# A decay floor moved into the scan, a fourth place for first loads, and four smaller edits in a gated-attention and two-MLP kernel

## The chip, the cores and the metric

The kernel runs on one core of a Trainium2 chip. A core has a matrix engine (TensorE, PE in the profile, with its weight loads shown apart as PEld), a vector engine (DVE), a scalar engine (ACT), a third engine (GpSimd, POOL) and a queue engine (SyncE, SP) that issues the DMA transfers here. The metric is device time in microseconds (us) of one execution of the whole program, lower is better. The time before is the median of three runs.

## The reference, cut to what matters

```python
def _attn_ref(q, k, v, alpha):              # q, k, v, alpha: 4 x 8 heads x 768 x 48
    for t in range(S):
        state = alpha[:, :, t, :, None] * state + np.einsum('bhd,bhe->bhde', k[:, :, t], v[:, :, t])
        y[:, :, t] = np.einsum('bhd,bhde->bhe', q[:, :, t], state)

def _moe_ref(x, mu_k, mu_r, w_k, w_v, w_r): # x: 4 x 768 x 384, w_k: 384 x 1024
    xk = mu_k * x + (1.0 - mu_k) * x_prev   # x_prev: x one token earlier
    xr = mu_r * x + (1.0 - mu_r) * x_prev
    k = np.maximum(xk @ w_k, 0.0)
    return sigmoid(xr @ w_r) * (k * k @ w_v)

def _moe2_ref(x, U, V, w_ch1, w_ch2):       # w_ch1: 384 x 1536
    u = x + (x.transpose(0, 2, 1) @ U @ V).transpose(0, 2, 1)
    return u + np.maximum(u @ w_ch1, 0.0) @ w_ch2
```

The three stages follow one another. The weights arrive as 64-bit floats; q, k, v and alpha as 32-bit.

## The kernel before

**Blocks.** The 4 x 768 tokens are cut into eight blocks of 384 tokens. A block goes through attention, then the first MLP (`moe1`); after all eight, the second MLP (`moe2`) goes through the eight blocks again. Every large product is done as three matmuls on a high and a low part of each operand (`mm3`), 384 columns wide; these are the 128x384 matmuls of the profile.

**Attention.** A block holds two units, a unit two phases (`ph`), a phase two heads: one head on partitions 0 to 47 (`EV`), the other on 64 to 111 (`OD`), together `BOTH` = 0 to 111. The time axis is cut into chunks of 128 tokens. `prep` (line 700) turns alpha into running products with two scans on DVE: a backward one into `G` and a forward one into `Fp`. Between them stands a floor: POOL takes the maximum of the three chunk starts of `G` and `DECAY_MIN` into `aC` (line 712), DVE takes its reciprocal into `bt` (line 713), and the second scan starts from that. Then come the transposes of the decayed keys (`keys_by_token`, PE, line 310), the score matmuls (`scores`), the state matmuls (`states`) and the outputs (`outputs`), whose results ACT copies into the block's `x`.

**The first block.** `first_attention` (line 826) does unit 1 before unit 0. Each phase is loaded into one of three places `T[0]` to `T[2]`; `tile_of` gives phases 2, 3, 0, 1 the places 0, 1, 2, 0, so the fourth load has to wait until the first phase is used up. The rows of x that don't fit a unit's own 96 partitions are spread by six small DMAs of 16 x 384 (`outputs`, `spread`), which read what unit 1 wrote. The copies of unit 0's outputs write all of rows 0 to 111, and so also the rows 48 to 63 that the spread fills; a spread DMA therefore comes after them.

**Weights.** `w_k` is loaded in pieces of 128, 256, 384, 128 and 128 columns into `raw` places, decoded by ACT and DVE to 32 bits (line 596), and split into high and low parts. `w_v`, `w_r` and the later weights go through four such places in turn, so a load waits until its place has been decoded.

**Results.** At the end of a block of `moe2`, DVE adds each of three 128-token results into a place of a ring of two (`x2_ring`) and SP sends it out: the third addition waits until the first result has left.

**What sets the order.** The kernel doesn't leave the order to the program text. `Plan` collects every operation with its operands and an assumed cost, and `schedule` (line 186) simulates five engines, each taking the ready operation of best priority; the priorities come from the table `DUE` and then from passes backward over the result (`issue`). Each engine runs its list strictly in that order. Where the simulation sees PE idle, it puts matmuls on a zero tile `warm` (128x128, line 395) that compute nothing; once placed, PE has to execute them. An assumed cost that is changed for one kind of operation (here the cost of a DMA, line 365) can therefore move instructions anywhere in the program.

## Time and profile before

| | |
|---|---|
| median of 3 runs | 724.15 us (722.25 to 725.62) |
| the profiled execution | 724.62 us, its span from first to last instruction 722.9 us |
| PE busy | 705.5 us (98%), 5319 instructions |
| DVE busy | 508.5 us (70%) |
| ACT busy | 354.5 us (49%) |
| POOL busy | 75.8 us (10%) |
| mean granted clock of PE | 0.992 |
| chain that ended last | PE 74%, DVE 6%, ACT 4%, DMA 3% |
| HBM | 43.85 MB read, 9.44 MB written |

A profile is one execution. Busy time of PE counts the matmuls on the zero tile too, so a PE that is busy 98% is not one that does useful work 98% of the time. In the timeline a row gives the start, the length, the engine, the source line, the operation with its output and input, the number of instructions merged into it, and in brackets how long the engine was idle just before and what ended that.

### The profile page before, as it was taken

To read this page: it belongs to the slowest core of one execution; us is meant where nothing else is said; L and a number is where in the kernel's file an instruction comes from. 1 tells how busy PE (TensorE), PEld (TensorE's weight loads), DVE (VectorE), ACT (ScalarE), POOL (GpSimd) and SP (SyncE) were. 2 spreads that over 40 slices of the span, in tenths; PEclk is the share of its full clock that TensorE was granted. 3 is DMA by queue.
4 is the path that set the end of the run, shared out by engine and by line. 5 is a ranking of instruction groups with operands and counts; after the bars stand their busy time and mean duration, and the time that the engine had idled before them with its cause. 6 is when DMAs were issued, how large, how long until landed. Compare 5 with 4: busy or idle time off the path is not lost.

```text
span 722.9 us, 13907 instructions
## 1 busy us (share of the span) xinstructions
PE 705.5 (98%) x5319; PEld 675.4 (93%) x5319; DVE 508.5 (70%) x1173; ACT 354.5 (49%) x901; POOL 75.8 (10%) x131
## 2 busy tenths in 40 slices
PE   7999999999999999999999999999999999999995
PEld 7798889899999999999999999999999999999995
DVE  6898987897776567773699999575665657474611
ACT  2588656976767557677797672212121112111210
POOL 2021101442130311311002100000000000000000
PEclk9999989999999999999999999999999999999998
DMA  8835733434333222313253240102020202020001
GB/s 222 200 102 157 186 84 102 108 94 109 85 98 75 63 62 60 98 51 99 65 153 110 66 143 16 51 0 66 1 67 1 65 1 67 1 66 2 34 1 37
DMA packets 29484, 55.46 MB, mean 77 GB/s; under 512 B 5344, under 2 KB 20064, under 8 KB 29408
## 3 DMA queue, kind: packets, MB, share of 16 engines
q1 hardware_dynamic: 29408, 54.48, 27.3%
q8 instruction: 43, 0.70, 0.4%
q14 instruction: 33, 0.27, 0.1%
HBM read 43.85 MB, written 9.44 MB: 74 GB/s over the span
## 4 chain that ended last, share of the span: by engine, by line
PE 74%; DVE 6%; ACT 4%; DMA 3%; issue 1%; SPq 1%; DVEq 0%; ACTq 0%
PE bank L305 73%; DMA arena<-in_qka_dram 3%; ACT arena L320 2%; DVE arena L137 2%; DVE arena L982 2%; DVE rounded L137 1%; PE bank L310 1%; SPq L366 1%; ACT rounded L320 1%; DVE shared L137 1%; ACT shared L320 1%; DMA out_dram<-arena 0%; ACT bank L320 0%; DVE shared L349 0%; DVEq L137 0%
## 5 line engine op out<-in xcount | busy, mean ns | idle before, releaser
L305 PE MATMUL bank<-rounded 128*128 128x384 f32 x2232 | 424.3, 339 | 2.9 <-ACT rounded L320 1.2
L305 PEld LDWEIGHTS bank<-rounded 128*128 128x128 f32 x2232 | 383.7, 186 | 13.2 <-ACT arena L320 2.2
L305 PE MATMUL bank<-rounded,shared 128*128 128x384 f32 x864 | 164.9, 335 | 0.8 <-DVE rounded L137 0.5
L320 ACT ACTIVATE rounded<-bank 128x384 fp32r<-128x384 f32 x160 | 78.3, 489 | 175.4 <-PE bank L305 174.3
L305 PEld LDWEIGHTS bank<-rounded,shared 128*128 128x128 f32 x864 | 150.9, 188 | 1.7 <-DVE rounded L137 1.0
L320 ACT ACTIVATE arena<-arena 128x384 f32<-128x384 f32 (+6 forms) x234 | 103.2, 463 | 48.2 <-DMA arena<-in_qka_dram 29.4
L137 DVE SCALAR_TENSOR_TENSOR rounded<-bank,rounded 128x384 fp32r<-128x384 f32 x96 | 53.4, 556 | 91.4 <-ACT rounded L320 90.3
L982 DVE STREAM_TRANSPOSE arena<-arena 32x96 f32<-32x96 f32 x384 | 103.8, 270 | 5.7
L305 PE MATMUL bank<-shared 128*48 128x128 f32 (+3 forms) x1472 | 100.3, 266 | 3.4 <-DMA shared<-in_v_dram 1.2
L305 PEld LDWEIGHTS bank<-shared 128*48 128x48 f32 (+2 forms) x1472 | 86.6, 142 | 17.8 <-issue 6.2
L320 ACT ACTIVATE rounded<-arena 128x384 fp32r<-128x384 f32 (+2 forms) x137 | 70.4, 522 | 63.6 <-DVE arena L982 49.4
L137 DVE SCALAR_TENSOR_TENSOR arena<-arena 128x384 int32<-128x384 int32 (+2 forms) x140 | 79.9, 590 | 8.9 <-ACT arena L320 8.3
L320 ACT ACTIVATE bank<-bank 128x384 f32<-128x384 f32 x128 | 61.6, 482 | 23.4 <-PE bank L305 22.7
L137 DVE TENSOR_TENSOR rounded<-arena,rounded 128x384 fp32r<-128x384 f32 (+1 forms) x108 | 60.5, 570 | 11.4 <-ACT rounded L320 10.9
L137 DVE TENSOR_TENSOR arena<-bank,arena 128x384 f32<-128x384 f32 (+1 forms) x76 | 41.5, 552 | 25.0 <-PE bank L305 9.9
L137 DVE TENSOR_TENSOR rounded<-bank,rounded 128x384 fp32r<-128x384 f32 x64 | 35.4, 552 | 30.6 <-ACT rounded L320 28.9
L320 ACT ACTIVATE arena<-bank 112x384 f32<-112x384 f32 (+3 forms) x76 | 37.3, 504 | 35.2 <-PE bank L305 33.3
L137 DVE TENSOR_TENSOR shared<-bank,arena 128x384 f32<-128x384 f32 x64 | 33.9, 547 | 24.5 <-PE bank L305 23.0
L137 POOL TENSOR_TENSOR rounded<-arena,rounded 128x384 fp32r<-128x384 f32 (+1 forms) x25 | 27.7, 1116 | 110.5 <-ACT rounded L320 110.4
L395 PE MATMUL bank<-warm 128*128 128x128 bf16 x581 | 37.4, 224 | 1.1 <-DVE arena L543 1.1
L395 PEld LDWEIGHTS <-warm 128*128 128x128 bf16 x581 | 34.5, 101 | 3.1 <-issue 1.5
L349 DVE TENSOR_TENSOR_SCAN shared<-arena 128x384 f32<-128x384 f32 x32 | 31.0, 967 | 4.4 <-ACT arena L320 4.3
(47 smaller groups left out, 258.3 us busy)
## 6 DMA issues: line engine op xcount, KB each, us to landing
arena<-in_qka_dram SPq DMA_DIRECT2D x56, 216.0 KB, 3.7
arena<-in_w_dram SPq DMA_DIRECT2D x24, 384.0 KB, 3.5
shared<-in_v_dram SPq DMA_DIRECT2D x32, 144.0 KB, 3.0
x2d<-arena SPq DMA_DIRECT2D x24, 192.0 KB, 2.2
arena<-x2d SPq DMA_DIRECT2D x8, 576.0 KB, 4.1
out_dram<-arena SPq DMA_DIRECT2D x24, 192.0 KB, 1.9
arena<-in_w_v_dram SPq DMA_DIRECT2D x8, 384.0 KB, 3.2
arena<-in_qka_dram SPq DMA_DIRECT2D x24, 72.0 KB, 2.0
```

The costliest lines, as they stand in the source:

```text
L137: fn(**args)
L305: "PE", cost, [out], [lhsT, rhs], lambda out, lhsT, rhs: fn(out, lhsT=lhsT, rhs=rhs, start=start, stop=stop),
L310: self.add("PE", cost, [out], [in_, ident], lambda: self.nc.tensor.transpose(out, in_, ident))
L320: self.add("ACT", cost, outs, [in_] + extra, lambda out, in_: fn(out, in_, func, **kw), out=out, in_=in_)
L349: lambda: self.nc.vector.tensor_tensor_scan(out=out, data0=d0, data1=d1, initial=0.0, op0=ALU.mult, op1=ALU.add), True,
L366: lambda: self.nc.sync.dma_start(out, in_),
L395: lambda i: nc.tensor.matmul(banks[SPARE[i]][:, 384:512], lhsT=warm, rhs=warm, start=True, stop=True), FILL_UNTIL, ROUNDS
L982: plan.dve(284, [to], [src], lambda to=to, src=src: nc.vector.transpose(out=to, in_=src))
```

## The change

Six edits, and the order that the planner makes of them:

- **Floor in the scan.** `ends` holds `DECAY_MIN` instead of zero off the chunk ends, the first element of a chunk is set to zero, and the backward scan takes the maximum where it took the sum. The result is already floored, so POOL's maximum and `aC` go: 32 instructions of line 712.
- **A fourth place.** `T[3]` lies on raw places 2 and 3. Phase 1 is loaded there, behind no other phase. All of `prep` now works on rows 0 to 111, so the second head is loaded with 48 rows instead of 64.
- **Outputs head by head.** In the first block unit 0's outputs are copied for each head alone (four copies of 48 x 384 on ACT instead of two of 112 x 384), which leaves the spread rows alone; the six spread DMAs now follow unit 1.
- **Smaller pieces.** `w_k` comes in pieces of 128, 128, 384, 128, 128 and 128 columns. Three are loaded from the start (four before), the last three later, and the due numbers `wk1` to `wk5` change.
- **Three result places.** `moe2` writes its results into `rs`, which has three places.
- **The planner's DMA cost** is the number of words over 56 instead of over 90.

The zero-tile matmuls in the program are 599 after, 581 before; PE's other instructions are the same 4001 matmuls in another order. Up to the first 128x384 matmul PE has 263 zero-tile matmuls now and had 325; between the first six 128x384 matmuls and the next transposes it has 240 and had 188.

```diff
@@ -41,7 +41,7 @@
 
 DUE = dict(
     slot1=2.01, end1=62, end2=81, end=28, keys=6.0, prep=1.66, load=52, mix_r=65, mix_k=44, mix0_r=61,
-    mix0_k=468, wk0=-238, wk1=-283, wk2=-17, wk3=45, wk4=60, wkk=7, wv=-12, r0=5, wr=37, early=31, x2=25, u=48, w1=227,
+    mix0_k=468, wk0=-238, wk1=-230, wk2=-220, wk3=38, wk4=45, wk5=60, wkk=7, wv=-12, r0=5, wr=37, early=31, x2=25, u=48, w1=227,
     w1s=-9, w2=23, pu=144, s_w="ACT DVE", s_lo="DVE", s_w1="ACT DVE", s_lo1="DVE",
     d1="ACT", d2="ACT", d="ACT", m0="DVE", m1="DVE", m="DVE", ut="DVE", ul="DVE",
     e0="DVE DVE", e1="DVE DVE", e2="DVE DVE", e="DVE POOL",
...
@@ -343,11 +343,11 @@
             self.nc.vector.tensor_scalar, True, out=out, in0=in0, scalar1=s1, scalar2=s2, **ops,
         )
 
-    def scan(self, out, d0, d1):
+    def scan(self, out, d0, d1, op=ALU.add):
         self.add(
             "DVE", 66.0 + 2.085 * out.free_size(), [out], [d0, d1],
             lambda: self.nc.vector.tensor_tensor_scan(
-                out=out, data0=d0, data1=d1, initial=0.0, op0=ALU.mult, op1=ALU.add
+                out=out, data0=d0, data1=d1, initial=0.0, op0=ALU.mult, op1=op
             ), True,
         )
 
...
@@ -362,7 +362,7 @@
         for d in out.shape:
             words *= d
         self.add(
-            "SP", max(cost, words / 90.0), [out if out_key is None else out_key], [in_ if in_key is None else in_key],
+            "SP", max(cost, words / 56.0), [out if out_key is None else out_key], [in_ if in_key is None else in_key],
             lambda: self.nc.sync.dma_start(out, in_),
         )
 
...
@@ -457,6 +457,7 @@
     Xs = [None, None]
     Xs[0] = new(KD + 1, TB + 1)
     raw_at = [words(arena, 2 * TB) for _ in range(4)]
+    T.append(view(arena, raw_at[2], (KD * TB + 1,)))
     raw_n = [0]
     rs_at = words(arena, NT * DM)
     rs = view(arena, rs_at, (NT, DM))
...
@@ -493,7 +494,6 @@
     KV = new(2, D, NC)
     carry = new(2, 2, D)
     G, Fp, bt = (att(TB) for _ in range(3))
-    aC = new(NC)
     w1h, w1l = (view(shared, i * KD * DF2, (KD, DF2), F32R) for i in range(2))
     last_w2 = [view(shared, 2 * KD * DF2 + i * DM, (DM,), F32R) for i in range(2)]
 
...
@@ -547,11 +547,12 @@
     plan.pool(600, [ident], [], lambda: make_identity(nc, ident))
 
     def make_ends():
-        nc.vector.memset(ends, 0.0)
+        nc.vector.memset(ends, DECAY_MIN)
         nc.vector.memset(ends[:, CH - 1 :: CH], 1.0)
 
     plan.dve(480, [ends], [], make_ends)
     plan.dve(400, [bt], [], lambda: nc.vector.memset(bt, 0.0))
+    plan.pool(60, [low], [], lambda: nc.gpsimd.memset(low, 0.0))
 
     def make_tri():
         nc.gpsimd.memset(tri, 1.0)
...
@@ -673,7 +674,7 @@
         return u // 4, (u // 2) % 2, (u % 2) * 2
 
     def tile_of(ph):
-        return T[{2: 0, 3: 1, 0: 2, 1: 0}[ph] if ph < 4 else ph % 3]
+        return T[{2: 0, 3: 1, 0: 2, 1: 3}[ph] if ph < 4 else ph % 3]
 
     def load_qka(ph, parts=((0, KD),), rows=D, to=None):
 
...
@@ -683,9 +684,10 @@
         for a, z in parts:
             for hh in range(2):
                 src = qka[b, h0 + hh, half, 0, a, 0]
+                n = D if hh else rows
                 plan.dma(
-                    t[64 * hh : 64 * hh + rows, a * TB : z * TB],
-                    bass.AP(src.tensor, src.offset, [[KD * TB, rows], [1, (z - a) * TB]]), in_key="in", cost=475.0,
+                    t[64 * hh : 64 * hh + n, a * TB : z * TB],
+                    bass.AP(src.tensor, src.offset, [[KD * TB, n], [1, (z - a) * TB]]), in_key="in", cost=475.0,
                 )
 
     def load_v(u):
...
@@ -694,30 +696,29 @@
             plan.dma(VS[u % 2][:, eo].rearrange("p c j d -> p (c j d)"), v[b, p0 // 2, half, eo], in_key="in")
 
     def check_pair(ph, t):
-        there = junk[:, 0 : t.free_size()].rearrange("p (c t) -> p c t", c=t.shape[1])
-        plan.act(there, t, AF.Relu, scale=-1.0, bias=ALPHA_MIN, accum_out=low[:, ph : ph + 1])
+        there = junk[BOTH, 0 : t.free_size()].rearrange("p (c t) -> p c t", c=t.shape[1])
+        plan.act(there, t, AF.Relu, scale=-1.0, bias=ALPHA_MIN, accum_out=low[BOTH, ph : ph + 1])
 
     def prep(ph, due, engs):
 
-        qt, kt, at = q_k_a(tile_of(ph))
-        g0, f, a0 = G[:, 0:TB:CH], fc[:, ph, :], firsts[:, ph, :]
+
+        qt, kt, at = (t[BOTH] for t in q_k_a(tile_of(ph)))
+        g, fp, f, a0, first = G[BOTH], Fp[BOTH], fc[BOTH, ph, :], firsts[BOTH, ph, :], at[:, 0:TB:CH]
         if ph >= CHECK_LATER:
             plan.at = due + 10
             check_pair(ph, at[:, 0:TB].rearrange("p (c t) -> p c t", t=CH)[:, :, 1:])
         plan.at = due
-        first = at[:, 0:TB:CH]
         plan.act(a0, first, AF.Copy)
-        plan.act(first, ends[:, 0:NC], AF.Copy)
-        plan.scan(G[:, ::-1], at[:, 1 : TB + 1][:, ::-1], ends[:, ::-1])
-        plan.pool(160, [aC], [g0], lambda: nc.gpsimd.tensor_scalar_max(out=aC, in0=g0, scalar1=DECAY_MIN))
-        plan.dve(110, [bt], [aC], lambda: nc.vector.reciprocal(bt[:, 0:TB:CH], aC))
-        plan.pool(163, [f], [a0, g0], lambda: nc.gpsimd.tensor_tensor(out=f, in0=a0, in1=g0, op=ALU.mult))
+        plan.act(first, ends[BOTH, 0:NC], AF.Copy, scale=0.0)
+        plan.scan(g[:, ::-1], at[:, 1 : TB + 1][:, ::-1], ends[BOTH, ::-1], ALU.max)
+        plan.dve(90, [bt], [g], lambda: nc.vector.reciprocal(bt[BOTH, 0:TB:CH], g[:, 0:TB:CH]))
+        plan.pool(163, [f], [a0, g], lambda: nc.gpsimd.tensor_tensor(out=f, in0=a0, in1=g[:, 0:TB:CH], op=ALU.mult))
         plan.at = due + 6
-        plan.scan(Fp, at[:, 0:TB], bt)
+        plan.scan(fp, at[:, 0:TB], bt[BOTH])
         plan.at = due + 14
-        plan.tt(KB[ph % 2], kt, G, ALU.mult, engs[0])
+        plan.tt(KB[ph % 2][BOTH], kt, g, ALU.mult, engs[0])
         plan.at = due + 17
-        plan.tt(QG[ph % 4], qt, Fp, ALU.mult, engs[1])
+        plan.tt(QG[ph % 4][BOTH], qt, fp, ALU.mult, engs[1])
 
     def scores(ph, due):
 
...
@@ -767,7 +768,8 @@
         if not half:
             plan.act(last, R[BOTH, :, :, NC - 1], AF.Copy)
 
-    def outputs(u, due, spread):
+    def outputs(u, due, spread, apart=False):
+
 
 
         b, half, p0 = unit(u)
...
@@ -788,7 +790,8 @@
                         else:
                             plan.mm(y, st[BOTH, h, j, c, :], QG[ph % 4][BOTH, cs], False, True, plan.S128)
         for j in range(2):
-            plan.act(x[BOTH, p0 + j, 1:], two_b[j][BOTH, 0:TB], AF.Copy)
+            for r in (EV, OD) if apart else (BOTH,):
+                plan.act(x[r, p0 + j, 1:], two_b[j][r, 0:TB], AF.Copy)
         if spread:
             for kk in range(KD):
                 for a in (0, 64):
...
@@ -840,7 +843,7 @@
                 keys_by_token(ph, due + 20 * j + 8)
                 scores(ph, due + 20 * j + 9)
             states(u, due + 25)
-            outputs(u, due + 30, i == 1)
+            outputs(u, due + 30, i == 0, i == 1)
 
 
     mm_at = [0]
...
@@ -1017,7 +1020,7 @@
         second(NF2 - 1)
         for t in range(NT):
             plan.at = mm_at[0] - EARLY + 4 * t
-            o = x2_ring()
+            o = rs[:, t, :]
             plan.tt(o, acc[t], u[:, t, :], ALU.add)
             tok = half * TB + t * P
             plan.dma(out[b, tok : tok + P, :], o, out_key=f"out{n}{t}")
...
@@ -1054,9 +1057,9 @@
     load_mu()
     c0 = 0
     for i, (n, at) in enumerate(
-        ((P, raw_at[0]), (2 * P, raw_at[1]), (3 * P, rs_at), (P, raw_at[3]), (P, raw_at[0]))
+        ((P, raw_at[0]), (P, raw_at[1]), (3 * P, rs_at), (P, raw_at[2]), (P, raw_at[3]), (P, raw_at[0]))
     ):
-        raw = load_weight(w_k[:, :, c0 : c0 + n], at, -1650 if i < 4 else DUE["wk4"] - 60)
+        raw = load_weight(w_k[:, :, c0 : c0 + n], at, -1650 if i < 3 else DUE[f"wk{i}"] - 60)
         for j in range(0, n, P):
             plan.at = DUE[f"wk{i}"] + DUE["wkk"] * (j // P)
             cs = slice(c0 + j, c0 + j + P)
```

On SP's queue at the start, before (`in_qka` are loads of q, k and alpha of one head, the widths 384, 768 and 1152 a part or all of the three; `in_v`, `in_mu`, `in_w_k` the other inputs; `arena<-arena` a spread DMA):

```order
L366 DMA arena<-in_qka_dram 64x1152 x2
L366 DMA shared<-in_v_dram 128x288 x3
L366 DMA arena<-in_qka_dram 64x1152 x2
L366 DMA shared<-in_v_dram 128x288
L366 DMA arena<-in_w_k_dram 128x3x256
L366 DMA arena<-in_w_k_dram 128x3x512
L366 DMA arena<-in_mu_dram 128x6
L366 DMA arena<-in_qka_dram 48x1152 x2
L366 DMA arena<-in_w_k_dram 128x3x768
L366 DMA arena<-arena 16x384 x3
```

and after, from the same place (behind the eight loads of phases 2 and 3):

```order
L366 DMA shared<-in_v_dram 128x288 x2
L366 DMA arena<-in_qka_dram 64x1152
L366 DMA arena<-in_qka_dram 48x1152
L366 DMA arena<-in_qka_dram 64x1152
L366 DMA arena<-in_qka_dram 48x1152
L366 DMA shared<-in_v_dram 128x288 x2
L366 DMA arena<-in_w_k_dram 128x3x256 x2
L366 DMA arena<-in_mu_dram 128x6
L366 DMA arena<-in_w_k_dram 128x3x768
L366 DMA arena<-arena 16x384 x6
```

The first two loads of v now go ahead of phase 0, phase 1 follows phase 0 directly, and all six spread DMAs stand in one row, ahead of the late pieces of `w_k`.

On DVE at the first phase, before (`SCALAR_TENSOR_TENSOR` of line 349 is a scan, line 137 the product with k or q):

```order
L349 SCALAR_TENSOR_TENSOR shared<-arena 128x384
L137 TENSOR_TENSOR shared<-arena,shared 128x384
L713 RECIPROCAL shared<-arena 128x3
L349 SCALAR_TENSOR_TENSOR shared<-arena,shared 128x384
L349 SCALAR_TENSOR_TENSOR shared<-arena 128x384
```

and after:

```order
L349 SCALAR_TENSOR_TENSOR shared<-arena 112x384
L714 RECIPROCAL shared<-shared 112x3
L137 TENSOR_TENSOR shared<-arena,shared 112x384
L349 SCALAR_TENSOR_TENSOR shared<-arena,shared 112x384
L349 SCALAR_TENSOR_TENSOR shared<-arena 112x384
```

The reciprocal reads the scan's own output and stands right behind it; the product comes third.

On PE at the end of the program, before (`bank0`, `bank1` and `bank2` collect the three results of the last block, `shared2` holds the last row of the second weight, so the row with it ends a result):

```order
L305 MATMUL bank0_73<-shared2_4057,rounded_71 128x384 x3
L305 MATMUL bank1_74<-rounded_71 128x384 x3
L305 MATMUL bank2_75<-rounded_71 128x384 x3
L305 MATMUL bank1_74<-rounded_71 128x384 x3
L305 MATMUL bank2_75<-rounded_71 128x384 x2
L305 MATMUL bank1_74<-shared2_4057,rounded_71 128x384 x3
L305 MATMUL bank2_75<-rounded_71 128x384
L305 MATMUL bank2_75<-shared2_4057,rounded_71 128x384 x3
```

and after:

```order
L305 MATMUL bank0_73<-shared2_4048,rounded_71 128x384 x3
L305 MATMUL bank1_74<-rounded_71 128x384
L305 MATMUL bank2_75<-rounded_71 128x384
L305 MATMUL bank1_74<-shared2_4048,rounded_71 128x384 x3
L305 MATMUL bank2_75<-rounded_71 128x384 x2
L305 MATMUL bank2_75<-shared2_4048,rounded_71 128x384 x3
```

The first result is complete with 10 matmuls still to come instead of 15.

On PE in the second block's attention, before (128x128 with `bank6` or `bank7` are scores of one head, three chunks; `bank0` to `bank2` products of the first MLP):

```order
L305 MATMUL bank6_79<-shared_72 128x128 x3
L305 MATMUL bank0_73<-rounded_71 128x384
L305 MATMUL bank7_80<-shared_72 128x128 x3
L305 MATMUL bank0_73<-rounded_71 128x384 x2
L305 MATMUL bank6_79<-shared_72 128x128 x3
L305 MATMUL bank1_74<-rounded_71 128x384
L305 MATMUL bank7_80<-shared_72 128x128 x3
L305 MATMUL bank1_74<-rounded_71 128x384 x2
L310 MATMUL bank5_78<-arena_70,shared_72 128x112 x3
```

and after, at the like place:

```order
L305 MATMUL bank6_79<-shared_72 128x128 x3
L305 MATMUL bank0_73<-rounded_71 128x384 x2
L305 MATMUL bank7_80<-shared_72 128x128 x3
L305 MATMUL bank1_74<-rounded_71 128x384 x2
L305 MATMUL bank2_75<-rounded_71 128x384 x2
```

Four groups of scores stood there with one, two and one products between them; now it is two groups with two between, and four products and six zero-tile matmuls behind.

## Rows read from the trace of the kernel before

**Rows 1.** Stretches of 20 us: length, PE, PEld, DVE, ACT, POOL busy (count), clock, DMA share, GB/s
```profile
0.00:20.00 20.00, 15.93 (x221) 14.63 (x222) 13.67 (x30) 6.61 (x22) 4.49 (x22) 1.00 0.87 225
20.00:40.00 20.00, 19.14 (x292) 17.08 (x293) 16.15 (x35) 11.72 (x32) 1.54 (x5) 1.00 0.73 187
40.00:60.00 20.00, 19.43 (x278) 18.29 (x276) 19.26 (x40) 17.07 (x43) 5.06 (x4) 1.00 0.41 117
480.00:500.00 20.00, 20.00 (x118) 20.00 (x117) 15.63 (x46) 4.33 (x9) 0.00 (x0) 1.00 0.20 60
```

**Rows 2.** The matmuls on the zero tile: the page's group, and one run in the timeline
```profile
L395 PE MATMUL bank<-warm 128*128 128x128 bf16 x581 | 37.4, 224 | 1.1 <-DVE arena L543 1.1
42.69 7.49 PE L395 MATMUL bank<-warm 128*128 128x128 bf16 x131
```

**Rows 3.** Timeline of PE in the first 95 us: rows with a wait
```profile
6.93 0.48 PE L310 MATMUL bank<-arena,shared 112*128 112x112 f32 x3 [0.97 <-DVE shared L713]
12.66 0.29 PE L305 MATMUL bank<-shared 128*48 128x48 f32 x2 [0.43 <-ACT shared L320]
14.18 0.74 PE L305 MATMUL bank<-shared 128*48 128x48 f32 x22 [1.23 <-DMA shared<-in_v_dram]
24.74 1.23 PE L305 MATMUL bank<-shared 48*128 48x128 f32 x12 [0.85 <-DVE arena L648]
41.01 0.62 PE L305 MATMUL bank<-rounded 128*128 128x384 f32 x2 [0.57 <-ACT rounded L320]
65.61 0.45 PE L305 MATMUL bank<-rounded 128*128 128x384 f32 x1 [0.61 <-ACT rounded L320]
66.74 3.23 PE L305 MATMUL bank<-rounded 128*128 128x384 f32 x17 [0.68 <-DVE rounded L137]
90.72 0.51 PE L310 MATMUL bank<-arena,shared 112*128 112x112 f32 x3 [0.53 <-ACT shared L320]
```

**Rows 4.** Timeline of the end: the last PE row and the last additions
```profile
712.54 0.56 DVE L137 TENSOR_TENSOR arena<-bank,arena 128x384 f32<-128x384 f32 x1 [0.65 <-PE bank L305]
714.95 0.69 PE L305 MATMUL bank<-shared,rounded 128*128 128x384 f32 x3
714.97 0.56 DVE L137 TENSOR_TENSOR arena<-bank,arena 128x384 f32<-128x384 f32 x1 [1.87 <-PE bank L305]
716.72 0.56 DVE L137 TENSOR_TENSOR arena<-bank,arena 128x384 f32<-128x384 f32 x1 [1.19 <-DMA out_dram<-arena]
```

**Rows 5.** Stretches of 2 us about the place where the clock fell
```profile
102.00:104.00 2.00, 2.00 (x11) 1.60 (x11) 1.61 (x4) 1.12 (x2) 0.00 (x0) 0.83 0.16 39
104.00:106.00 2.00, 2.00 (x9) 1.68 (x9) 1.48 (x4) 0.00 (x0) 0.38 (x2) 0.50 0.57 155
110.00:112.00 2.00, 2.00 (x19) 1.56 (x16) 0.40 (x1) 1.34 (x5) 0.00 (x0) 0.96 0.21 59
```

**Rows 6.** Timeline of PE there: two of the score rows, 48 rows of the array each
```profile
99.45 0.93 PE L305 MATMUL bank<-shared 48*128 48x128 f32 x6
103.33 1.64 PE L305 MATMUL bank<-shared 48*128 48x128 f32 x6
```

**Rows 7.** Timeline of DVE and POOL at the first phase: scan, floor, reciprocal
```profile
4.73 0.96 DVE L349 TENSOR_TENSOR_SCAN shared<-arena 128x384 f32<-128x384 f32 x1 [0.85 <-ACT arena L320]
5.78 0.23 POOL L712 TENSOR_SCALAR arena<-shared 128x3 f32<-128x3 f32 x1 [2.60 <-DVE shared L349]
6.71 0.17 DVE L713 RECIPROCAL shared<-arena 128x3 f32<-128x3 f32 x1
```

**Rows 8.** Timeline of SP and ACT: loads of the first block and who waited
```profile
14.21 1.30 SPq L366 DMA_DIRECT2D arena<-in_qka_dram  x2
17.34 0.45 ACT L320 ACTIVATE arena<-arena 128x3 f32<-128x3 f32 x2 [1.83 <-DMA arena<-in_qka_dram]
33.60 0.49 ACT L320 ACTIVATE arena<-bank 112x384 f32<-112x384 f32 x1
36.07 0.21 ACT L320 ACTIVATE arena<-arena 128x3 f32<-128x3 f32 x1 [1.47 <-DMA arena<-in_qka_dram]
61.98 11.80 SPq L366 DMA_DIRECT2D arena<-in_w_v_dram  x5
```

28 lines of the change are left out of this document (14 added, 14 removed).

## The prediction

> **What bounds the kernel now.** I read the stretches first. From about 95 us on PE has no gap worth naming: 20.00 us busy of 20.00 in a stretch of the second MLP [rows 1]. There time falls only if PE's own work shrinks, and the change leaves its 4001 matmuls as they are. The first 60 us look as full (15.93, 19.14 and 19.43 of 20), but the next view takes that back: 581 matmuls run on the zero tile, 37.4 us busy [rows 2], all before 74 us. They are the room that the planner saw in front of PE. What can be won is therefore these matmuls, the real waits left between them, and the end. The waits are in PE's timeline [rows 3]: ten of 0.39 us or more from 6.93 to 90.72, 6.65 us together (two of 0.39 are not shown). Third, the end: the last addition starts 1.19 us late, released by the transfer of the first result [rows 4]. Last, the clock: it is at half speed for some 7 us near 104 us [rows 5].
>
> **The change part by part.** *Zero-tile matmuls.* One costs 7.49 / 131 = 0.057 us [rows 2]. The program holds 18 more, and PE must execute them whether or not the data are there: 18 x 0.057 = **+1.0 us**. They sit elsewhere: 62 fewer before the first wide product (3.5 us), 52 more right behind its first six (3.0 us). So data that come earlier for the first products help little; PE then runs through 240 zero-tile matmuls, 13.7 us.
>
> *Loads and spread.* Phase 1's load was issued at 14.21, behind two pieces of `w_k`, and ACT waited until 17.34 for it [rows 8]; now it follows phase 0. The loads of v go two places forward, and PE's 1.23 us at 14.18 waited on one of them. The spread's last DMA followed the copy at 33.60 and ACT waited until 36.07 [rows 8]; now all six follow unit 1. I let four waits go with that: 0.43, 1.23, 0.85 and 0.57 us [rows 3], **-3.1 us**. The 0.97 at the start, before any of this, stays, as do the others: those at 65 to 91 us come from later loads, which nothing speeds up. The start is then 1.0 - 3.1 = **-2.1 us**. Bounds: with all ten waits gone -5.6; with none gone and the four shown or counted after 60 us (0.61, 0.68, 0.39, 0.53 = 2.2) once more, +3.2. I stay near the middle because the zero-tile matmuls are certain and the waits are only partly tied to the loads that move.
>
> *Floor in the scan.* The scan ended at 5.69, the reciprocal came at 6.71 [rows 7], with POOL's 0.23 us and two handovers between. But the product with the keys stood in that gap anyway, so DVE saves about 0.1 us a phase. Later phases are hidden by a full PE; if that cover were gone, a phase would gain 1.0 us. Priced at nothing. A scan with a maximum has no row; I take a scan's 0.96 us for it (bound: the shorter products at 0.56 below, the same 0.4 above, in the first block four times, -1.6 to +1.6), since both scans combine two inputs element after element.
>
> *Head by head.* Two more copies on ACT, 0.49 us each [rows 8], 1.0 us while ACT is busy 11.72 of 20 [rows 1]: nothing, or 1.0 us if the output copies were the last thing that the mix waits for.
>
> *Smaller pieces and the planner's cost.* The bytes are the same; one more DMA to issue on SP, about 0.6 us (1.30 for two [rows 8]), hidden while SP waits. The late pieces stand behind the six spread DMAs, so they wait for unit 1's copies; phase 4's loads queue behind them and the next attention waits for those. Priced at nothing, its failure is a rival.
>
> *Three results.* The first two additions start 0.03 us after their matmuls; the last matmul ends at 714.95 + 0.69 = 715.64, the last addition starts at 716.72 [rows 4]. Without the wait it starts at 715.68: **-1.0 us**. If the three transfers, now closer together, slow one another, this shrinks to 0.
>
> The sum is 724.6 - 2.1 - 1.0 = 721.5 us against the profiled execution. That one lay 0.5 us above the median, so the forecast for a median is **721.0 us**. It keeps one fall of the clock.
>
> **The rivals.** *The clock holds.* From 102 to 112 us the granted clock was 0.83, three stretches at 0.50 (the first is shown), and 0.96 [rows 5]: 2 x 0.17 + 6 x 0.50 + 2 x 0.04 = 3.4 us lost, between its two levels, 2.4 and 1.2 GHz. PE was busy 2.00 of 2.00. Before the fall it ran score matmuls on 48 rows in groups of three (0.93 us for one at 99.45, 1.64 us for the like one at 103.33 [rows 6]), with one or two wide products between. The new order has two such groups there and then four products. If the clock holds, 721.0 - 3.4 = 717.6 us. Against it: attention with as few wide products stands elsewhere, and nothing shows which of these places tips. The Trainium skill (TensorE: Matmul & The Clock Gate, Part 1: The HAM clock gate) says that an idle engine is throttled and a busy one released. By that rule a PE kept full by zero-tile matmuls never falls, and the time would be this rival's; rows 5 disagree, since PE was not idle when it fell.
>
> *The clock falls twice*, in two of the attention stretches: 721.0 + 3.4 = 724.4 us.
>
> *The start gives nothing.* The zero-tile matmuls stand in the way and new waits replace the four: 721.0 + 3.1 = 724.1 us, only the end is won.
>
> *Slower: SP's queue.* SP stood 11.80 us over five loads of `w_v` [rows 8], each waiting for a place; PE lost only 0.61 and 0.68 us then. Now late `w_k` pieces, spread and phase loads share that queue with `w_v`, and DVE, which decodes them, has no room: 19.26 of 20 [rows 1]. If PE waits out half of such a stretch, it costs 5.9 us: 721.0 + 5.9 = 726.9 us. It decides the sign from 3.1 us of new waits on.
>
> **How the numbers follow.** Chances: forecast 0.38, clock holds 0.32, SP's queue 0.15, nothing at the start 0.08, two falls 0.07. The forecast's start term is uncertain by some 1.5 us either way. A measurement here can tell about 0.5%, 3.6 us, from no change, so faster means below 720.5 and slower above 727.8. Faster takes nearly all of the clock case (0.30) and a third of the forecast (0.13): 0.43. Slower takes half of the queue's case and a tail of two falls: 0.11. The rest, 0.46, is within. The range of 8 in 10 goes from 716.0 (the clock case with 1.6 us more at the start) to 726.5 (most of the queue's case lies above it). The forecast's own range is 719 to 723.
>
> **What would show it.** In the new profile: 599 zero-tile matmuls at about 0.057 us; waits of PE in the first 95 us of 3 to 4 us; no wait for `in_v` near 14 us; ACT's wait for phase 1 gone by 15 us; reciprocals right behind the scans, no line of POOL's maximum; the last addition 0.05 us after the last matmul; the granted clock at one place or none at 0.50. I am wrong if PE waits over 6 us in the first 95, if a gap appears where 20.00 of 20 stood, or if the last transfers land later though the additions are earlier.

## The result, and the profile after

The changed kernel takes **713.46 us** (median of 4 runs, 712.08 to 714.28), the kernel before 723.21 us beside it (722.25 to 725.62). The ratio is 0.9858, with an interval of 0.9826 to 0.9891: about 10 us faster. The prediction was 721.0 us with a range of 716.0 to 726.5; the time lies 2.5 us under that range.

The profiled execution went from 724.62 to 714.28 us, its span from 722.9 to 712.6, so 10.3 us are to be found in the trace. The stretches first, as in [rows 1]: length, then busy time (and count) of PE, PEld, DVE, ACT and POOL, the granted clock, the DMA share and GB/s.

```profile
0.00:20.00 20.00, 18.93 (x255) 17.28 (x256) 15.89 (x36) 6.87 (x23) 4.14 (x21) 1.00 0.85 228
20.00:40.00 20.00, 20.00 (x320) 18.55 (x318) 16.61 (x34) 15.58 (x38) 0.04 (x1) 1.00 0.62 160
40.00:60.00 20.00, 20.00 (x263) 19.63 (x261) 19.57 (x40) 17.73 (x50) 3.94 (x5) 1.00 0.58 171
480.00:500.00 20.00, 20.00 (x117) 20.00 (x117) 9.61 (x26) 4.47 (x9) 0.00 (x0) 1.00 0.16 50
```

From 20 to 60 us PE is full, where it had 19.14 and 19.43 of 20. Its timeline has only these waits left, after the one at the very start (1.07 us); in the first 96 us none of the ten of [rows 3] remains.

```profile
145.26 0.51 PE L310 MATMUL bank<-arena,shared 112*128 112x112 f32 x3 [0.33 <-ACT shared L320]
374.94 1.34 PE L305 MATMUL bank<-rounded 128*128 128x384 f32 x6 [0.41 <-ACT rounded L320]
438.37 0.62 PE L305 MATMUL bank<-rounded,shared 128*128 128x384 f32 x2 [1.26 <-ACT rounded L320]
439.32 1.94 PE L305 MATMUL bank<-rounded,shared 128*128 128x384 f32 x7 [0.34 <-DVE rounded L137]
```

The matmuls on the zero tile, answering [rows 2], are 18 more, as the order had told; PE is busy with them for 2.3 us more, where 1.0 was forecast. The first run is 1.2 us of that: 59 took 6.12 us, where 57 took 4.91 in the kernel before.

```profile
L395 PE MATMUL bank<-warm 128*128 128x128 bf16 x599 | 39.7, 228 | 1.1 <-DVE arena L543 1.1
1.07 6.12 PE L395 MATMUL bank<-warm 128*128 128x128 bf16 x59 [1.07 <-DVE arena L543]
```

That is pace and not number: from 4 to 6 us after the start PE did 25 of them here and 36 in the kernel before, and in another kernel below (a_poolmax) the same 59 took 5.13 us. It bought nothing either way, for the first transposes start at 7.02 us now and started at 6.93, behind the wait of 0.97 us [rows 3]: that wait is filled, not won. The other 1.1 us are the 18 matmuls. PE's other instructions are 4738 in both traces (5319 less 581, 5337 less 599), not the 4001 written further up; that they are the same number is what the argument needs.

The end, answering [rows 4]: the last row of PE ends at 705.64 + 0.69 = 706.33, and the last addition starts 0.04 us later, released by PE.

```profile
705.50 0.56 DVE L137 TENSOR_TENSOR arena<-bank,arena 128x384 f32<-128x384 f32 x1 [0.31 <-PE bank L305]
705.64 0.69 PE L305 MATMUL bank<-shared,rounded 128*128 128x384 f32 x3
706.37 0.56 DVE L137 TENSOR_TENSOR arena<-bank,arena 128x384 f32<-128x384 f32 x1 [0.31 <-PE bank L305]
```

The clock, answering [rows 5]: near 104 us it now holds, and it falls at 440, for half as long: 2 x 0.46 + 2 x 0.39 = 1.7 us lost, where it was 3.4.

```profile
438.00:440.00 2.00, 1.30 (x6) 0.97 (x7) 1.97 (x5) 0.31 (x1) 0.00 (x0) 1.00 0.38 140
440.00:442.00 2.00, 2.00 (x8) 2.00 (x7) 0.98 (x5) 0.32 (x1) 0.00 (x0) 0.54 0.75 135
442.00:444.00 2.00, 2.00 (x9) 2.00 (x9) 0.56 (x1) 0.17 (x1) 0.00 (x0) 0.61 0.82 313
```

One mark divides the program: the transfer of the first result. These two rows of SP's queue are of the kernel before and of the changed one.

```profile
449.79 1.28 SPq L366 DMA_DIRECT2D out_dram<-arena  x2
```
```profile
438.37 0.82 SPq L366 DMA_DIRECT2D out_dram<-arena  x2
```

Up to it the change gains 11.4 us. From there to PE's end it gives 2.1 back (265.85 before, 267.96 after; 1.7 of it is the clock), and from PE's end to the end of the span it gains 1.0 (7.26 and 6.27). In the first part the listed waits shrink by 6.5 us and the clock's loss by 3.4, and the zero-tile matmuls add 2.3: 7.6 us. The other 3.8 us lie in PE's busy time of its other products; the page's rows by shape overlap one another and don't place them.

A part of the gain is the clock, and it varies from one execution to the next. Of the kernel before, 64 executions beside the experiments are counted (one more, of 864.77 us at a clock of 0.748, is left out): the 8 with a mean granted clock of at least 0.997 took 719.3 to 723.2 us, 721.6 on average, the 21 with at most 0.990 took 723.1 to 728.9. The four of the changed kernel had 0.996 to 0.998, and the two with 0.997 and 0.998 took 712.8 and 712.1. At a like clock, then, some 9 of the 10 us are left.

### The profile page after: what moved, and what is told of

It reads as the page before. It is cut to its first block, busy times and chain, and to the rows that moved or that the text cites. A ratio compares the mean times of both kernels' runs of the same rounds, so it can differ in the third digit from the quotient of the medians.

```text
span 712.6 us, 13923 instructions
## 1 busy us (share of the span) xinstructions
PE 702.8 (99%) x5337; PEld 674.2 (95%) x5337; DVE 507.3 (71%) x1173; ACT 354.7 (50%) x903; POOL 65.0 (9%) x101
## 4 chain that ended last, share of the span: by engine, by line
PE 92%; DVE 5%; ACT 1%; issue 1%; DMA 1%; POOL 0%; SPq 0%; DVEq 0%; ACTq 0%
PE bank L305 85%; PE bank L395 5%; DVE arena L985 2%; DVE arena L137 2%; PE bank L310 1%; DVE rounded L137 1%; DMA arena<-in_qka_dram 1%; ACT arena L320 1%; ACT rounded L320 0%; POOL shared L137 0%; ACT bank L320 0%; DVE shared L137 0%; ACT shared L320 0%; POOL arena L715 0%; SPq L366 0%
## 5 line engine op out<-in xcount | busy, mean ns | idle before, releaser
L305 PEld LDWEIGHTS bank<-rounded,shared 128*128 128x128 f32 x864 | 152.5, 190 | 2.3 <-ACT rounded L320 1.6
L320 ACT ACTIVATE arena<-arena 128x384 f32<-128x384 f32 (+5 forms) x234 | 101.7, 461 | 23.8 <-DMA arena<-in_qka_dram 14.8
L305 PE MATMUL bank<-shared 128*48 128x128 f32 (+3 forms) x1472 | 96.5, 262 | 0.1
L305 PEld LDWEIGHTS bank<-shared 128*48 128x48 f32 (+2 forms) x1472 | 82.1, 140 | 14.7 <-issue 6.7
L320 ACT ACTIVATE arena<-bank 112x384 f32<-112x384 f32 (+4 forms) x78 | 37.8, 503 | 39.3 <-PE bank L305 38.4
L395 PE MATMUL bank<-warm 128*128 128x128 bf16 x599 | 39.7, 228 | 1.1 <-DVE arena L543 1.1
L395 PEld LDWEIGHTS <-warm 128*128 128x128 bf16 x599 | 36.6, 102 | 3.2 <-issue 1.9
L137 DVE TENSOR_TENSOR shared<-arena,shared 112x384 f32<-112x384 f32 (+1 forms) x57 | 31.5, 558 | 1.9 <-ACT shared L320 1.0
## 6 DMA issues: line engine op xcount, KB each, us to landing
arena<-in_qka_dram SPq DMA_DIRECT2D x58, 216.0 KB, 3.9
arena<-in_w_dram SPq DMA_DIRECT2D x24, 384.0 KB, 3.3
arena<-in_w_v_dram SPq DMA_DIRECT2D x8, 384.0 KB, 3.3
arena<-in_w_k_dram SPq DMA_DIRECT2D x5, 384.0 KB, 7.4
```

Source lines behind the costliest of these rows:

```text
L137: fn(**args)
L305: "PE", cost, [out], [lhsT, rhs], lambda out, lhsT, rhs: fn(out, lhsT=lhsT, rhs=rhs, start=start, stop=stop),
L320: self.add("ACT", cost, outs, [in_] + extra, lambda out, in_: fn(out, in_, func, **kw), out=out, in_=in_)
L395: lambda i: nc.tensor.matmul(banks[SPARE[i]][:, 384:512], lhsT=warm, rhs=warm, start=True, stop=True), FILL_UNTIL, ROUNDS
```

## The experiments

In the names, b_ is the kernel before with something added, a_ the changed kernel with something altered. Times are medians. The ratio is to the kernel before, run beside it (medians 722.4 to 724.9 us); it is not the quotient of the two medians and can differ from it by 0.002. The columns behind it: zero-tile matmuls in the program; PE's waits between 3 and 96 us, summed; ACT's waits for loads of q, k and a over the whole span; DVE's busy time in the first 100 us; the start of the first result's transfer. The last four are of one execution each.

| kernel | us | ratio [95%] | zero tile | PE waits | ACT waits | DVE | first result |
|---|---|---|---|---|---|---|---|
| before | 723.21 | 1 | 581 | 6.65 | 29.4 | 83.97 | 449.79 |
| changed | 713.46 | 0.9858 [0.9826, 0.9891] | 599 | 0 | 14.8 | 90.26 | 438.37 |
| b_cost | 714.06 | 0.9843 [0.9808, 0.9877] | 596 | 0.65 | 15.1 | 89.22 | 438.60 |
| a_cost90 | 722.35 | 0.9981 [0.9956, 1.0006] | 520 | 7.42 | 34.9 | 84.01 | 448.73 |
| a_place3 | 715.00 | 0.9856 [0.9816, 0.9896] | 575 | 2.79 | 14.1 | 87.87 | 441.44 |
| b_results | 722.17 | 0.9969 [0.9941, 0.9998] | 581 | 4.09 | 28.2 | 83.98 | 448.51 |
| b_cost_in | 717.17 | 0.9904 [0.9868, 0.9940] | 578 | 1.14 | 20.9 | 87.43 | 439.68 |
| b_cost_w | 723.88 | 0.9990 [0.9968, 1.0012] | 562 | 2.92 | 32.1 | 85.13 | 446.84 |
| b_cost40 | 724.45 | 1.0009 [0.9993, 1.0025] | 727 | 1.64 | 5.3 | 79.88 | 450.58 |
| b_cost70 | 720.02 | 0.9940 [0.9916, 0.9963] | 573 | 2.42 | 19.2 | 84.96 | 444.13 |
| b_cost_results | 713.15 | 0.9839 [0.9803, 0.9874] | 596 | 1.10 | 16.2 | 88.66 | 439.39 |
| b_lat24 | 710.74 | 0.9814 [0.9777, 0.9850] | 597 | 0 | 7.7 | 89.04 | 436.37 |
| b_lat30 | 717.39 | 0.9928 [0.9906, 0.9949] | 600 | 0.66 | 6.9 | 87.29 | 442.66 |
| b90_lat28 | 741.55 | 1.0248 [1.0203, 1.0294] | 591 | 4.81 | 15.0 | 83.58 | 446.71 |
| a_lat24 | 715.79 | 0.9909 [0.9881, 0.9937] | 590 | 0 | 7.8 | 89.07 | 441.36 |
| a_poolmax | 713.42 | 0.9847 [0.9810, 0.9883] | 599 | 0.67 | 16.2 | 88.55 | 439.95 |
| a_nofill | 716.18 | 0.9893 [0.9855, 0.9930] | 0 | 29.18 | 12.6 | 88.00 | 439.95 |

### Which part did it

The trace of before, read again, gave a theory. From 60 to 100 us ACT waits six times for loads of q, k and a, 7.56 us together; these are the first and the third. Columns: start, duration, engine and line, output from input, and in brackets the wait and its releaser.

```profile
62.54 0.21 ACT L320 ACTIVATE arena<-arena 128x3 f32<-128x3 f32 x1 [1.69 <-DMA arena<-in_qka_dram]
83.97 0.45 ACT L320 ACTIVATE arena<-arena 128x3 f32<-128x3 f32 x2 [0.82 <-DMA arena<-in_qka_dram]
```

Behind the first stands the decoding of weights, for which DVE waits:

```profile
65.22 0.56 DVE L137 TENSOR_TENSOR rounded<-arena,rounded 128x384 fp32r<-128x384 f32 x1 [2.12 <-ACT rounded L320]
```

Then PE waits, at 65.61 and 66.74 [rows 3]. ACT carries its instructions out in their order, and the planner had put a phase's copies where it believed the load landed. Its belief is one number, words per ns, and the change makes it smaller.

**b_cost** is that number alone:

```diff
-            "SP", max(cost, words / 90.0), ...
+            "SP", max(cost, words / 56.0), ...
```

> The kernel before with one number changed: the planner's time for a transfer, words / 56 in place of words / 90. Theory (the number did it): with 90 the planner believes that a load is there before it is, puts ACT's copies for that load ahead of the weights' decoding, and ACT stands before them (six waits for in_qka from 62.54 to 94.61 us, 7.6 us together); DVE waits for ACT (2.12 us at 65.22) and PE for both. With 56 these waits go: PE's waits of the first 95 us from 6.65 to under 2 us, and the time about 717 us (ratio 0.992). Rival (the loads did it: the fourth place and the smaller pieces): this kernel stays within 1.5 us of the kernel before and keeps ACT's waits for in_qka. Second rival (any other order would have done): time between 718 and 728, waits in other places, their sum as large.

714.06 us: all but 0.6 us of the gain, and faster than the 717 expected. From 60 to 100 us ACT waits once for such a load, 0.69 us, and over the whole span 15.1 us, where it was 29.4. The last number of the page's row of ACT's copies has it, before and in b_cost:

```profile
L320 ACT ACTIVATE arena<-arena 128x384 f32<-128x384 f32 (+6 forms) x234 | 103.2, 463 | 48.2 <-DMA arena<-in_qka_dram 29.4
```
```profile
L320 ACT ACTIVATE arena<-arena 128x384 f32<-128x384 f32 (+5 forms) x234 | 101.9, 462 | 26.9 <-DMA arena<-in_qka_dram 15.1
```

The copy that had waited 1.69 us at 62.54 starts without a wait in b_cost; from 59.82 us up to it ACT carries out nine other instructions.

```profile
63.33 0.22 ACT L320 ACTIVATE arena<-arena 128x3 f32<-128x3 f32 x1
```

**a_cost90** is the changed kernel with the number set back:

```diff
-            "SP", max(cost, words / 56.0), ...
+            "SP", max(cost, words / 90.0), ...
```

> The changed kernel with that number alone set back to 90. Theory (the number did it): ACT's waits for in_qka after 60 us return, and PE's waits in the first 95 us with them, 4 us or more: about 719 to 721 us (0.995). Rival (the loads did it): it stays at 713 to 715 us. Second rival (any other order): no direction is foretold, but the sum of PE's waits in the first 95 us doesn't follow the number.

722.35 us, a little above the 719 to 721 expected. The five other parts together give 0.2%, with an interval that takes in zero; PE's waits are back at 7.42 us, ACT's for in_qka from 60 to 100 us at 7.67 and over the whole span at 34.9. The rival of the loads falls. Of the other, any other order, this much falls: the waits follow the number. How much of the time is a lucky order comes back further down.

**a_place3** is the changed kernel without the fourth place and its pieces, with the old due numbers of the pieces (their line, and the one that says how many pieces are loaded from the start, are not shown):

```diff
-    T.append(view(arena, raw_at[2], (KD * TB + 1,)))
-        return T[{2: 0, 3: 1, 0: 2, 1: 3}[ph] if ph < 4 else ph % 3]
+        return T[{2: 0, 3: 1, 0: 2, 1: 0}[ph] if ph < 4 else ph % 3]
-        ((P, raw_at[0]), (P, raw_at[1]), (3 * P, rs_at), (P, raw_at[2]), (P, raw_at[3]), (P, raw_at[0]))
+        ((P, raw_at[0]), (2 * P, raw_at[1]), (3 * P, rs_at), (P, raw_at[3]), (P, raw_at[0]))
```

> The changed kernel with three places for the first loads, the old five pieces of w_k and their old due times. Theory (the number did it): phase 1's load waits again for the place of an earlier phase and ACT for it before 20 us, but PE bridges that with zero-tile matmuls and catches up by 60 us: within 1.5 us of the changed kernel, 713 to 715. Rival (the loads did it): 717 us or more, with waits of PE over 3 us in the first 95.

715.00 us, 1.5 more than the changed kernel by the medians and nothing by the ratios; the executions overlap (713.2 to 716.9 and 712.1 to 714.3), so whether the fourth place is worth anything is not told apart. The rival's 717 us are not reached. 2.79 us of waits came back, so waits alone are not the measure.

**b_results** is three places alone:

```diff
-            o = x2_ring()
+            o = rs[:, t, :]
```

> The kernel before with the last sums written into three places in place of two. The last addition no longer waits for the first result's transfer and starts 0.05 us after the last matmul, where it was 1.07: 1.0 us faster (0.9986), the rest of the trace as before. Rival: the three transfers, now closer together, slow one another and the span ends where it did, 0.0. Second rival: rs is in use by the loads of the next steps, which the planner then moves: another sign, with PE's waits changed far from the end.

Ratio 0.9969: 0.1 to 4.3 us faster, which holds the 1.0 expected; from PE's end to the end of the span it is 6.2 us, where it was 7.26. In the first 300 us every engine carries out the same instructions in the same order as in the kernel before, yet the listed waits went from 6.65 to 4.09, and the clock fell at 16 and at 104 us, where it had fallen at 103 alone: that much two executions of one order differ.

```profile
16.00:18.00 2.00, 2.00 (x16) 1.80 (x14) 0.76 (x1) 0.16 (x2) 0.00 (x0) 0.50 1.09 341
```

### Which loads, and is it a matter of the right number

**b_cost_in** gives the new number to the loads of q, k, a and v alone, **b_cost_w** to the weights' loads alone (`"w"` in place of `"in"`):

```diff
+            "SP", max(cost, words / (56.0 if in_key == "in" else 90.0)), ...
```

> The kernel before with words / 56 for the loads of q, k, a and v alone; the weights' loads stay at words / 90. Theory (ACT's copies of a phase stood before loads that had not landed): these loads are what ACT waited for, so this half of the number brings most of the gain: PE waits 0 to 2 us between 3 and 96 us, ACT waits under 2 us for in_qka after 60 us, time 714 to 718 us. Rival (the queue filled with weights set the order): it stays at 721 to 724 us, and the gain comes with the weights' loads.

> The kernel before with words / 56 for the weights' loads alone; q, k, a and v stay at words / 90. Theory (ACT's copies of a phase): it stays within 3 us of the kernel before, and ACT's waits for in_qka after 60 us stay at 5 us or more. Rival (the queue filled with weights): 714 to 718 us with these waits gone, since the planner then sees the weights' loads hold up the phases' loads behind them.

717.17 and 723.88 us. The loads that ACT waited for carry most of the gain, the weights' loads by themselves none. ACT's waits from 60 to 100 us are not as clean: 4.1 us remain in the first (expected under 2), 3.3 in the second (expected 5 or more). Over the whole span they are 20.9 and 32.1 us, against 29.4 before: only the first shrinks.

**b_cost40** and **b_cost70** put other numbers there:

```diff
+            "SP", max(cost, words / 40.0), ...
```

> The kernel before with words / 40. Theory (a load must not be planned earlier than it lands): a price above the one of the change is as good, 712 to 717 us, with few waits of PE before 96 us; more zero-tile matmuls take their place. Rival (56 gave a lucky order, any other number is as likely to be slower): the time lies anywhere from 714 to 727, with waits over 4 us again.

724.45 us; the theory as written fell. PE waits little, but there are 727 zero-tile matmuls (not the 740 that the next expectation has) in place of 596, and they took 9 us more of PE (38.4 in b_cost):

```profile
L395 PE MATMUL bank<-warm 128*128 128x128 bf16 x727 | 47.6, 225 | 1.0 <-DVE arena L543 1.0
```

With the transfers priced that high the planner put work late and filled PE in front of it. DVE shows it best. Its busy time in the first 100 us is the third number with a count in these rows, of before, of b_cost and of b_cost40:

```profile
0.00:100.00 100.00, 92.30 (x1151) 83.40 (x1152) 83.97 (x173) 63.35 (x175) 13.49 (x39) 1.00 0.64 163
```
```profile
0.00:100.00 100.00, 98.26 (x1219) 89.22 (x1220) 89.22 (x185) 66.53 (x182) 14.69 (x41) 1.00 0.61 168
```
```profile
0.00:100.00 100.00, 96.75 (x1249) 88.84 (x1251) 79.88 (x163) 59.88 (x159) 10.32 (x37) 1.00 0.57 152
```

DVE decodes the weights and prepares the phases. In the kernel before it stood idle for 16.0 of its first 100 us, in b_cost for 10.8. So the theory became: the time is least where the price is near what the loads take.

> The kernel before with words / 70, between 90 (723.8 us) and 56 (714.1); words / 40 had given 724.5 with 740 zero-tile matmuls and 1.6 us of waits before 96 us. Theory (the time has its least where the price is near what the loads take: below it PE waits, above it the planner leaves room and fills it with zero-tile matmuls): 715 to 720 us, PE waits of 1 to 4 us between 3 and 96 us. Rival (each number gives an order of its own, without a trend): it is as likely above 722 as below.

720.02 us, at the edge of the 715 to 720 expected and between its neighbours, with 2.42 us of waits: 723.2, 720.0, 714.1, 724.5 for 90, 70, 56, 40. These four alone were tried, and orders with like waits differ by some us (below), so where between 70 and 40 the least lies is not settled. That 56 is near what the loads take can be read from the trace of before: 56 words per ns are 224 GB/s, and in the first 20 us, with the DMA engines 0.87 busy, 225 GB/s moved [rows 1]. 90 words per ns are 360 GB/s.

### The end, and a kernel that beats both

**b_cost_results** joins the number and the three places.

> The kernel before with words / 56 and with three places for the last sums, nothing else of the change. In the kernel with words / 56 alone PE ended at 704.50 us, the last addition waited 3.19 us for the first result's transfer and started at 707.41. With a place of its own it starts 0.04 us after the last matmul: 2.9 us less, about 711.2 us, 2 us faster than the changed kernel: then the other three parts of the change (floor in the scan, fourth place with its pieces, outputs head by head) give nothing or cost a little. Rival (these parts give something on their own): this kernel stays at or above 713.5 us.

713.15 us, 1.9 more than expected (0.9 of it a later end of PE than in b_cost) and just under the rival's 713.5, so neither is borne out; but it is no slower than the changed kernel. Floor in the scan, fourth place with its pieces, and outputs head by head together give nothing that shows. In b_cost the last addition had waited longer than in before, for the first result's transfer:

```profile
703.66 0.56 DVE L137 TENSOR_TENSOR arena<-bank,arena 128x384 f32<-128x384 f32 x1 [1.70 <-PE bank L305]
707.41 0.56 DVE L137 TENSOR_TENSOR arena<-bank,arena 128x384 f32<-128x384 f32 x1 [3.19 <-DMA out_dram<-arena]
```

Here it is gone:

```profile
705.46 0.56 DVE L137 TENSOR_TENSOR arena<-bank,arena 128x384 f32<-128x384 f32 x1 [0.31 <-PE bank L305]
```

The page of before gives the median time from issue to landing (last column) of one load of q, k and a, and the planner still has it at 1.0 + 1.9 = 2.9 us:

```profile
arena<-in_qka_dram SPq DMA_DIRECT2D x56, 216.0 KB, 3.7
```

**b_lat24** is b_cost_results with the planner's fixed time raised:

```diff
-    LAT = {..., "SP": 1900.0}   (and the same in TO_PE and OWN)
+    LAT = {..., "SP": 2400.0}
```

> The kernel with words / 56 and three places for the last sums (713.15 us), and the planner's fixed time from a transfer's issue to its use raised from 1900 to 2400 ns: a load of one head's q, k and a is then planned at 2.9 + 0.5 = 3.4 us, where the trace shows 3.7 to 3.9. Theory (nearer to the trace is better): ACT's waits for in_qka, 8.0 us in all, shrink to under 6 and the time is 711 to 713 us. Rival (the optimum is past, as with words / 40): more than 640 zero-tile matmuls, 715 us or more.

710.74 us (710.12 to 711.27): 2.7 us under the changed kernel and the best of all. ACT's waits for in_qka went from 8.0 to 6.6 us in the first 100 (under 6 was expected) and from 16.2 to 7.7 over the whole span, and PE has no listed wait between 3 and 372 us.

Three more runs asked whether that is a law or a lucky order. **b_lat30** has 3000 ns there, **a_lat24** is the changed kernel with 2400, and **b90_lat28** has the fixed time at 2800 and the rate left at 90.

> The kernel with words / 56, three places for the last sums and 3000 ns in place of 2400 from issue to use: a load of q, k and a is planned at 4.0 us, behind the 3.6 to 3.9 of the traces. Theory (least where the plan agrees with the trace): no longer better than with 2400 ns, 711 to 716 us. Rival (later is always better): under 709.5 us. Second rival (2400 gave a lucky order): 713 to 722 us with PE waits over 2 us before 96 us.

> The changed kernel with 2400 ns in place of 1900 from issue to use. Theory (nearer to the trace is better): the same step gave 2.4 us on the kernel with words / 56 and three places, so 710 to 712.5 us. Rival (a lucky order there): 712.5 to 718 us, with PE waits of more than 1 us before 96 us or a wait and a fall of the clock elsewhere.

> The kernel before with three places for the last sums, the rate left at words / 90 and the planner's fixed time from issue to use raised from 1900 to 2800 ns: a load of one head's q, k and a is then planned at 0.6 + 2.8 = 3.4 us, as in the kernel that took 710.74 us with words / 56 and 2400 ns. Theory (what counts is when a single load lands): 710 to 715 us, DVE busy 88 us or more in the first 100. Rival (what counts is how fast a queue of loads moves, which the fixed time doesn't show): 717 to 723 us, DVE busy 84 to 87 us.

717.39 us for 3000: it turns back, though by a little more than expected, and with 0.66 us of waits where the lucky order should have had over 2. 715.79 us for 2400 on the changed kernel: 2.3 slower, not faster, which is the rival's time without its signs: no wait before 96 us and no fall of the clock. So the step from 1900 to 2400 is not a gain by itself. b_lat24 and a_lat24 are 5.0 us apart with like waits, and the page's rows put it in attention's small products, the same 1472 with the same mean time, but 5.2 us more of PE in a_lat24 (the second row). Why they pack worse in its order is not shown.

```profile
L305 PE MATMUL bank<-shared 128*48 128x128 f32 (+3 forms) x1472 | 95.6, 262 | 0.0
```
```profile
L305 PE MATMUL bank<-shared 128*48 128x128 f32 (+3 forms) x1472 | 100.8, 263 | 0.0
```

An order can thus be a few us better or worse by luck, and that of b_lat24 may be a lucky one.

741.55 us for the fixed time without the rate, outside both ranges. Its start is nearer to the rival's: DVE 83.58 and the first result at 446.71, a gain of 2 us against b_results where the rate gave 9. That speaks for what the rival says, that it counts how fast a queue of loads is planned to move, but does not show it: this start also has a wait of PE of 3.84 us at 15.89, with the clock at half speed from 14 to 24 us. Most of the loss against b_results is three waits of 5.7 us in the second MLP, with the clock at half speed for 6.8 us about each; before the first ended, DVE had 16 STREAM_TRANSPOSE to do ahead of the addition that PE waited for:

```profile
485.05 4.53 DVE L982 STREAM_TRANSPOSE arena<-arena 32x96 f32<-32x96 f32 x16
```
```profile
490.40 0.69 PE L305 MATMUL bank<-rounded 128*128 128x384 f32 x1 [5.75 <-DVE arena L137]
```

### The floor, and the zero tile

**a_poolmax** takes the floor on POOL again (not shown: the place `aC`, the zeros in `ends` and the copy that sets a chunk's first element are as before too):

```diff
-        plan.scan(g[:, ::-1], at[:, 1 : TB + 1][:, ::-1], ends[BOTH, ::-1], ALU.max)
-        plan.dve(90, [bt], [g], ... reciprocal(bt[BOTH, 0:TB:CH], g[:, 0:TB:CH]))
+        plan.scan(g[:, ::-1], at[:, 1 : TB + 1][:, ::-1], ends[BOTH, ::-1])
+        plan.pool(160, [aC], [g], ... tensor_scalar_max(out=aC[BOTH], in0=g[:, 0:TB:CH], scalar1=DECAY_MIN))
+        plan.dve(110, [bt], [aC], ... reciprocal(bt[BOTH, 0:TB:CH], aC[BOTH]))
```

> The changed kernel with the floor taken by POOL's maximum behind an adding scan, as before. The scan with a maximum took 0.946 us and the adding one 0.967, so the operation is no dearer. Theory (PE is full, and the gap of 1.0 us between scan and reciprocal is hidden): within 1.5 us of the changed kernel, 712 to 715 us. Rival (the shorter chain of the first block is part of the gain): 716 us or more, with PE waits before 30 us.

713.42 us, the changed kernel's time: the floor in the scan is worth nothing that shows here.

**a_nofill** leaves out the matmuls on the zero tile, which write no result:

```diff
-FILL_UNTIL = 100000.0
+FILL_UNTIL = 0.0
```

> The changed kernel without its 599 zero-tile matmuls in the program's order. Theory (they only stand where PE would wait for data, 41 us in all before 103 us): PE waits about 35 to 41 us instead, the clock starts at half speed and falls again between, and since the first block's matmuls then run at 1.2 GHz on a PE that is not the bound there, it costs 1 to 5 us: 714 to 719 us. Rival (they stand in the way of work whose data are there, as the prediction's +1.0 us for 18 of them has it): 708 to 712 us.

716.18 us: 2.7 us slower, as the theory had it. PE waits 29.2 us instead (35 to 41 were expected), and its clock is at half speed for most of 32 to 53 us. Taken together, the 599 gain more than they cost. What 18 more or fewer cost is not shown by it, since without them the clock changes too.

## Why the prediction was wrong, point by point

**The step that failed** is one sentence: the planner's cost was "priced at nothing". It was read as bookkeeping of an order that the change shows anyway; but that number makes the order, and alone it took the kernel from 723.77 to 714.06 us, while the changed kernel without it took 722.35. The views held the answer. Rows 1 showed 225 GB/s at a DMA share of 0.87 where the planner reckoned with 360, and rows 8 showed ACT's waits for the phases' loads.

**The waits.** Four of ten were let go, -3.1 us, and the later ones kept because they "come from later loads, which nothing speeds up". All ten went, 6.65 us, though the first of them was filled and not won. Nothing did speed the loads up: the median for one of 216.0 KB was 3.7 us before and is 3.9 after. The copies that waited for them were put behind other work of ACT. Of the start's bounds, -5.6 to +3.2, the lower one was this case. By itself it makes 717.5 us, which the range holds; with the clock's 1.7 us it is 715.8, just under it, and the rest is PE's shorter busy time, for which the sum had no term.

**DVE.** The rival on SP's queue took DVE's 19.26 of 20 [rows 1] for an engine without room. Over 100 us it had 16.0 us idle, and 6.3 of these went to work (9.7 idle after). PE waited for none of it.

**Zero-tile matmuls.** The price, +1.0, measured +2.3 in PE's busy time, 1.1 without the slower pace of the first run. But that they are only a cost was wrong: most stand where PE would wait, and without any the time is 2.7 us longer.

**The clock.** The forecast kept one fall of 3.4 us; it moved to 440 us and cost 1.7. In b_cost, b_cost_in, b_cost40, b_cost70, b_cost_results, b_lat24 and a_poolmax it did not fall at all between 5 and 704 us. The rival was the right mechanism in part, at another place. Its reason, that the order of the score matmuls decides, is not borne out: in b_results the clock fell at other places in the same order.

**Three results** were right: 1.0 predicted, 1.0 measured at the end, with the 0.04 us foretold.

**Floor, head by head, smaller pieces** were right at nothing as far as they were told apart: the scan with a maximum took 0.946 us on average and the adding one on the same 112 rows 0.949 (a_poolmax), so the bound of 1.6 us either way was not needed. The reciprocal follows the scan at once, answering [rows 7]:

```profile
4.26 0.96 DVE L349 TENSOR_TENSOR_SCAN shared<-arena 112x384 f32<-112x384 f32 x1 [0.36 <-issue]
5.25 0.18 DVE L714 RECIPROCAL shared<-shared 112x3 f32<-112x3 f32 x1
```

Head by head was not run alone.

**Of the signs**, these came true: the 599 matmuls, no wait for in_v near 14 us, no line of POOL's maximum, the last addition right behind the last matmul, and one place with a low clock. PE's waits of 3 to 4 us in the first 95 did not: there are none. Nor is ACT's wait for phase 1 gone by 15 us: the fourth such wait is still there, at 16.27 (it was 17.34 in [rows 8]), and cost PE nothing.

```profile
16.27 0.44 ACT L320 ACTIVATE arena<-arena 112x3 f32<-112x3 f32 x2 [1.58 <-DMA arena<-in_qka_dram]
```

**What stays open.** The sum of the measured terms is 7.0 us (waits and clock over the whole span -6.6 and -1.7, zero tile +2.3, end -1.0); the other 3.3 us are shorter busy time of PE's other products, and no run named their cause. Nor was it settled why the same small products of attention take 5.2 us more of PE in one order than in another (b_lat24 and a_lat24), so it is open too how much of the 10 us is luck of the order; that the gain comes and goes with the number, by 8 us or more both ways, is above that.

## What to carry to other kernels

Where a planner sets the order, its prices are part of the kernel: hold each against the trace (GB/s of a stretch with busy DMA engines, the median from issue to landing) before any edit of the work itself. Too cheap a transfer shows as in-order engines that wait for loads, with others waiting behind them; too dear a one shows as filler and late work on an engine whose wait list is nearly empty. Here, with 90, 70, 56 and 40 words per ns, ACT's waits fell from 29.4 to 19.2, 15.1 and 5.3 us, and the time only as far as the third. An engine that is full in one stretch is judged over the whole stage, since its idle time upstream is what a better order spends.
